# Attention of a gated recurrence with its MLP: from 128-token chunks on the whole tensor array to 64-token sub-chunks on its quarters

## The chip, the cores and the metric

One NeuronCore of one Trainium2 chip runs the program. The metric is device time in microseconds, the median of three executions. Engines named below: TensorE (PE for its products, PEld for its weight loads), VectorE (DVE), ScalarE (ACT), GpSimd (POOL) and SyncE (SP), which issues the transfers.

## The reference

Attention with a decaying state, for 4 batches, 8 heads, 768 tokens and a head size of 48, then one block of token mixing and an MLP (model size 384, hidden size 1536):

```python
for t in range(S):
    kt, vt, rt = (k[:, :, t], v[:, :, t], r[:, :, t])
    cur = np.einsum('bhd,bhe->bhde', u[None] * kt, vt)
    y[:, :, t] = np.einsum('bhd,bhde->bhe', rt, state + cur)
    state = w[None, :, :, None] * state + np.einsum('bhd,bhe->bhde', kt, vt)
...
xt = x.transpose(0, 2, 1)
h = xt @ U @ V
u = x + h.transpose(0, 2, 1)
ch = np.maximum(u @ w_ch1, 0.0) @ w_ch2
return (u + ch).astype(np.float32)
```

x is y with its heads side by side. All data are float32, except that the MLP's weights may arrive as float64.

## The kernel before

A batch is six chunks of 128 tokens. Inside a chunk the recurrence is written as products: r and k are multiplied by powers of the decay w and their inverses (`tables`, the tables `tab`, `tabr`, `tabT`), so that a chunk's output is (masked scores) times v, plus r times the state at the chunk's start, plus a diagonal term with u. For chunk n the functions are:

- `a_load`, `a_load_blocks` (L250, L266): r, k, v with tokens on partitions, and from batch 1 on r and k again as 32 x 32 blocks, which VectorE turns.
- `a_pre` (L288): ks (k times the table) and dv (the diagonal term) on GpSimd.
- `a_tr_r`, `a_tr_k` (L335, L357): r and k with head dimensions on partitions, two heads (96 rows) at a time. From batch 1 on the scores use float32r operands, so r and k are each split into a high and a low part (L351 and L353, L371 and L372). r is spread to a block form (`bm`, zeros in the other head's rows), so that one product gives two heads.
- `a_sc` (L376): the scores, in three float32r products per pair of heads (L388 to L390), in batch 0 one float32 product (L383); then the causal mask (L397).
- `a_sq` (L404): r times the state. `a_av` (L413): masked scores times v, added to it in PSUM, then x (L430).
- `a_su` (L442): k times v for the next state, added and decayed at L457 and L458.
- `a_g`, `g_units`, `c_g`, `c_u`: x times U, and the gates that make u of x. `c_store`, `c_blocks`, `c_turn`: u goes to memory and comes back as blocks that VectorE turns.
- `m_1`, `m_2` (L607, L623): the MLP, in two blocks of 384 tokens and twelve hidden steps of 128, each product as three float32r products on high and low parts. 24 steps of 18 products (L613 to L615, L631 to L633) make a batch.

The order of the work is written by hand as lists of units. Batch 0's attention is merged with the conversion of the first 12 weight units (L833). After it, the loop at L840 places the units of batch b's MLP on a line from 0 to 1 and spreads the units of batch b+1's attention over the first 0.6 to 0.7 of it (`add`, L844). `within` (L654) lets the list of a batch run on into the next batch's first chunks. The program's scheduler works from this order, with the estimated times of each instruction; `queued` ties a unit behind given instructions. PSUM has eight banks: tags mm (2), acc (3), tr, sc and av (1 each).

## Time and profile before

| | |
|---|---|
| time, median of 3 runs | 494.33 us (492.8 to 495.66) |
| profiled execution: span from first to last instruction | 492.1 us |
| mean granted TensorE clock in it | 0.968 |
| TensorE busy, products and loads | 461.5 us and 446.6 us |
| VectorE, ScalarE, GpSimd busy | 303.3, 149.6, 235.6 us |
| DMA | 45.23 MB in 196880 packets |

The profile names instructions by engine and line of the kernel. A row of a group holds: line, engine, operation, output <- inputs, shapes, count, then busy time in us and the mean ns of one, then the idle time ahead of it and what ended that. PE is the matmul, PEld the weight load of the same product. Matmuls are pipelined: the length of one in the trace holds its way through the array, so what a product costs in a stream is the distance of starts. A float32 product stands in the trace as two loads and two matmuls, a float32r product as one of each. Times are from the span's start. The profiled execution's own time beyond its span is not given; the median of the runs lies 2.2 us above it.

### The profile page before, as it was taken

How to read it: one execution, taken by the hardware profiler on the slowest of the kernel's cores; microseconds unless marked ns; L12 is line 12 of the kernel's file. 1: busy time of each engine (PE TensorE's matmuls, PEld its weight loads, DVE VectorE, ACT ScalarE, POOL GpSimd, SP SyncE). 2: the span in 40 equal slices, each digit the busy share in tenths (PEclk: the TensorE clock that was granted, in tenths of full speed). 3: DMA queues.
4: the chain of work that ended last, by engine and by line, in shares of the span. 5: the costliest groups of instructions: out<-in, count | busy, mean ns of one | idle time of the engine just before them, and what ended most of it. 6: DMA issues, size and time to landing. Idle time of an engine off the chain costs nothing.

```text
span 492.1 us, 7932 instructions
## 1 busy us (share of the span) xinstructions
PE 461.5 (94%) x2891; PEld 446.6 (91%) x2891; DVE 303.3 (62%) x543; ACT 149.6 (30%) x290; POOL 235.6 (48%) x227
## 2 busy tenths in 40 slices
PE   7869878979999999999999999999999999999994
PEld 6858757969998989999999999999999999999994
DVE  7998968997788666837677453676672533213112
ACT  3535524434332232333222322323231222211110
POOL 5957565747978571645777602468751021000000
PEclk9977969999999999999999999999999999999998
DMA  9999704554764663676267225542001152001001
GB/s 159 200 312 405 160 17 73 89 82 74 103 113 95 101 102 90 152 107 97 50 96 140 54 66 108 107 75 50 2 0 49 57 113 73 0 1 48 1 0 55
DMA packets 196880, 45.23 MB, mean 92 GB/s; under 512 B 187682, under 2 KB 193571, under 8 KB 196835
## 3 DMA queue, kind: packets, MB, share of 16 engines
q1 hardware_dynamic: 196834, 44.66, 44.2%
q8 instruction: 25, 0.41, 0.4%
q14 instruction: 21, 0.16, 0.1%
HBM read 35.79 MB, written 8.85 MB: 91 GB/s over the span
## 4 chain that ended last, share of the span: by engine, by line
PE 64%; DVE 14%; POOL 7%; issue 6%; SPq 4%; DMA 3%; ACT 1%; DVEq 0%; POOLq 0%; ACTq 0%
PE p L631 8%; PE p L632 8%; PE p L613 8%; PE p L633 8%; PE p L615 8%; PE p L614 8%; PE pav L421 5%; SPq L275 3%; DVE rl L353 2%; PE pav L410 2%; DVE raw_w L189 2%; POOL kT L323 2%; PE psu L449 2%; DVE raw_w L188 1%; POOL dv L295 1%
## 5 line engine op out<-in xcount | busy, mean ns | idle before, releaser
L619 DVE SCALAR_TENSOR_TENSOR hl<-p,hh 128x384 fp32r<-128x384 f32 x96 | 52.6, 549 | 102.1 <-ACT hh L618 102.0
L613 PE MATMUL p<-uTh,w1s 128*128 128x384 f32 x288 | 98.3, 344 | 2.8 <-DVE hl L619 2.5
L631 PE MATMUL p<-w2s,hh 128*128 128x384 f32 x288 | 98.5, 342 | 1.4 <-ACT hh L618 1.4
L614 PE MATMUL p<-uTl,w1s 128*128 128x384 f32 x288 | 97.7, 339 | 1.2 <-DVE uTl L546 1.2
L615 PE MATMUL p<-uTh,w1s 128*128 128x384 f32 x288 | 97.3, 338 | 0.0
L632 PE MATMUL p<-w2s,hh 128*128 128x384 f32 x288 | 96.7, 336 | 0.0
L618 ACT ACTIVATE hh<-p 128x384 fp32r<-128x384 f32 x96 | 46.7, 489 | 148.5 <-PE p L615 147.3
L633 PE MATMUL p<-w2s,hl 128*128 128x384 f32 x288 | 78.8, 338 | 0.1
L613 PEld LDWEIGHTS p<-uTh,w1s 128*128 128x128 f32 x288 | 54.4, 189 | 4.6 <-DVE hl L619 3.7
L631 PEld LDWEIGHTS p<-w2s,hh 128*128 128x128 f32 x288 | 54.2, 188 | 2.6 <-ACT hh L618 2.4
L614 PEld LDWEIGHTS p<-uTl,w1s 128*128 128x128 f32 x288 | 54.6, 190 | 2.0 <-DVE uTl L546 2.0
L615 PEld LDWEIGHTS p<-uTh,w1s 128*128 128x128 f32 x288 | 54.5, 189 | 0.0
L632 PEld LDWEIGHTS p<-w2s,hh 128*128 128x128 f32 x288 | 54.2, 188 | 0.0
L601 POOL TENSOR_TENSOR uTl<-ut,uTh 128x384 fp32r<-128x384 f32 x21 | 21.5, 1025 | 66.6 <-ACT uTh L600 65.2
L633 PEld LDWEIGHTS p<-w2s,hl 128*128 128x128 f32 x288 | 52.5, 189 | 0.5 <-DVE hl L619 0.2
L323 POOL TENSOR_TENSOR kT<-kT,tabT 96x512 f32<-96x512 f32 x18 | 27.3, 1518 | 42.0 <-DVE kT L321 32.7
L421 PEld LDWEIGHTS pav<-ldv,am 128*128 128x128 f32 x320 | 43.4, 198 | 1.5 <-DVE am L397 1.5
L421 PE MATMUL pav<-ldv,am 128*128 128x48 f32 x320 | 42.8, 272 | 0.6 <-DVE am L397 0.5
L397 DVE TENSOR_TENSOR am<-psc,mask 128x512 f32<-128x512 f32 x45 | 30.5, 678 | 9.7 <-PE psc L390 8.0
L353 DVE SCALAR_TENSOR_TENSOR rl<-rT,bm,rh 96x512 fp32r<-96x512 f32 x36 | 34.1, 959 | 3.9 <-ACT rh L351 3.9
L351 ACT ACTIVATE rh<-rT,bm 96x512 fp32r<-96x512 f32 x36 | 24.1, 716 | 22.8 <-POOL rT L323 22.6
L323 POOL TENSOR_TENSOR rT<-rT,tabT 96x512 f32<-96x512 f32 x18 | 24.8, 1379 | 10.8 <-DVE rT L321 10.7
(142 smaller groups left out, 766.6 us busy)
## 6 DMA issues: line engine op xcount, KB each, us to landing
raw_w<-in_moe_w_ch_dram SPq DMA_DIRECT2D x24, 384.0 KB, 7.8
out_dram<-x SPq DMA_DIRECT2D x24, 192.0 KB, 2.1
ud<-x SPq DMA_DIRECT2D x21, 192.0 KB, 2.0
ub<-ud SPq DMA_DIRECT2D x84, 48.0 KB, 2.3
ldr<-in_r_dram SPq DMA_DIRECT2D x20, 192.0 KB, 3.2
ldk<-in_k_dram SPq DMA_DIRECT2D x20, 192.0 KB, 4.0
ldv<-in_v_dram SPq DMA_DIRECT2D x20, 192.0 KB, 3.1
bl<-in_r_dram SPq DMA_DIRECT2D x48, 48.0 KB, 2.4
```

The source lines that it names most:

```text
L323: nc.gpsimd.tensor_mul(xT, xT, tabT[:, i])
L353: nc.vector.scalar_tensor_tensor(rl[:, :, j, :], rT, bm[:, j, 0:1], f32(rh[:, :, j, :]), ALU.mult, ALU.subtract)
L397: nc.vector.tensor_tensor(am, pt.rearrange("p (h t) -> p h t", h=4), mask.unsqueeze(1).broadcast_to([128, 4, C]), ALU.mult)
L421: nc.tensor.matmul(avp[n][:, h * D:(h + 1) * D], lhsT=am[:, hh, :], rhs=vt[:, h, :], start=(c == 0 and h == 0), stop=(h == H - 1), skip_gr ...
L613: nc.tensor.matmul(pt, lhsT=wt[:, 0, fs], rhs=uh[:, ct, :], start=(ct == 0), stop=False)
L614: nc.tensor.matmul(pt, lhsT=wt[:, 0, fs], rhs=ul[:, ct, :], start=False, stop=False)
L615: nc.tensor.matmul(pt, lhsT=wt[:, 1, fs], rhs=uh[:, ct, :], start=False, stop=(ct == NCT - 1))
L618: i_hh = nc.scalar.activation(hh, pt, AF.Relu)
L619: i_hl = nc.vector.scalar_tensor_tensor(hl, pt, 0.0, f32(hh), ALU.max, ALU.subtract)
L631: nc.tensor.matmul(pt, lhsT=hh[:, ts_], rhs=W2[f][:, 0], start=(f == 0), stop=False)
L632: nc.tensor.matmul(pt, lhsT=hh[:, ts_], rhs=W2[f][:, 1], start=False, stop=False)
L633: nc.tensor.matmul(pt, lhsT=hl[:, ts_], rhs=W2[f][:, 0], start=False, stop=(f == NFT - 1))
```

## The change

A chunk of 128 tokens is handled as two sub-chunks of 64, with a state for each. A pair of heads lies on rows 0 to 47 and 64 to 111, so that each head has one half of the array's rows. Every product of the attention then uses 64 rows and 64 columns of the array at most:

- scores only within a sub-chunk (`p_sc`), in float32 for all batches: the splits of r and k and the block form of r are gone, and the mask has 64 columns;
- k times v per sub-chunk (`p_su`), and two states per chunk (`a_st`);
- scores times v and r times the state per sub-chunk (`p_out`). For the second head of each pair v is needed with its two token halves exchanged; `load_swapped` loads it so, in two more transfers per chunk.

A chunk's output is made in two parts (`a_part`): row 0 uses the array's upper rows for the output while the next chunk's second scores and state products use the lower rows; row 1 the other way round. `in_turn` issues the two lists alternately, each product tied behind the one before. Between the two parts stands a product on the whole array (`whole` takes the next MLP product for it, or `between` makes one), and the second part's first product waits for a small ScalarE read of the bank (`see`, `behind`), as both parts write to one bank. `a_first` makes the scores and state products of a batch's first chunk. Chunks are made ready (`ready`) two ahead. A batch's list now begins with its own loads and ends with its last chunk. In batch 0 weight conversions are queued behind the last mask and the last state (`gate`).

```diff
-    PD = 2 * D
+    HP = 64
+    C2 = C // 2
+    PD = HP + D
+    PE_ = 2 * HP
     DM = H * D
...
+    def load_swapped(n):
+        b, c = divmod(n, NCH)
+        t = work.tile([128, NP, D], F32, tag="vsw", name=f"vsw_{n}", bufs=NVS)
+        for i in range(2):
+            s0 = c * C + i * C2
+            nc.sync.dma_start(t[(1 - i) * C2:(2 - i) * C2], v[b, 1::2, s0:s0 + C2, :].rearrange("h p d -> p h d"))
+        vsw[n] = t
+    vsw = {}
...
+    def p_sc(n, j):
+        rT, kT = trs[n]
+        pt = abs_[n][j]
+        rows = head_rows(j)
+        return [lambda q=q, i=i: nc.tensor.matmul(
+            pt[(i ^ j) * C2:(i ^ j) * C2 + C2, q * C2:(q + 1) * C2], lhsT=kT[rows, q, i * C2:(i + 1) * C2],
+            rhs=rT[rows, q, i * C2:(i + 1) * C2], start=True, stop=True) for q in range(NP) for i in range(2)]
+    def p_su(n, i):
+        if n % NCH == NCH - 1 and i:
+            return []
+        ks, vt, dv = pre[n]
+        pt = abs_[n][i]
+        half = slice(i * C2, (i + 1) * C2)
+        hp = HP if n < NCH else D
+        def one(q, j):
+            m = D if j else HP
+            k0 = (2 * q + j) * hp
+            return nc.tensor.matmul(pt[j * HP:j * HP + m, SU + q * D:SU + (q + 1) * D],
+                                    lhsT=ks.rearrange("p h d -> p (h d)")[half, k0:k0 + m],
+                                    rhs=vt[half, 2 * q + j, :], start=True, stop=True)
+        return [lambda q=q, j=j: one(q, j) for q in range(NP) for j in range(2)]
+    def p_out(n, row):
+        am = ams[n]
+        vt = pre[n][1]
+        rT = trs[n][0]
+        pt = avp[n]
+        ps_ = []
+        def to(q, j, i):
+            return pt[i * C2:(i + 1) * C2, (2 * q + j) * D:(2 * q + j + 1) * D]
+        def av(q, j, i):
+            half = slice(row * C2, (row + 1) * C2)
+            return nc.tensor.matmul(to(q, j, i), lhsT=am[j][half, q, :],
+                                    rhs=vsw[n][half, q, :] if j else vt[half, 2 * q, :],
+                                    start=(row == 0 and q == 0), stop=False, skip_group_check=True)
+        def sq(q, i):
+            rows = head_rows(row)
+            return nc.tensor.matmul(to(q, row, i), lhsT=rT[rows, q, i * C2:(i + 1) * C2], rhs=St[n, i][rows, q, :],
+                                    start=False, stop=(row == 1 and q == NP - 1), skip_group_check=True)
+        for q in range(NP):
+            for i in range(2):
+                ps_.append(lambda q=q, i=i: av(q, i ^ row, i))
+        for q in range(NP):
+            for i in range(2):
+                if (n, i) in St:
+                    ps_.append(lambda q=q, i=i: sq(q, i))
+        return ps_
+    def in_turn(last, *lists):
+        for k in range(max(map(len, lists))):
+            for l in lists:
+                if k < len(l):
+                    with ExitStack() as st:
+                        if last is not None:
+                            st.enter_context(tc.issue_after(last.ins))
+                        last = l[k]()
+        return last
+    SU = 4 * C2
...
+    def whole(*args, **kw):
+        if not opened:
+            return nc.tensor.matmul(*args, **kw)
+        with tc.issue_after(opened.pop()):
+            closed.append(nc.tensor.matmul(*args, **kw))
+    def a_banks(n):
+        abs_[n] = [ps_tile(t, f"pab_{n}_{j}", 1) for j, t in enumerate(AB)]
+    def between(n):
+        if opened:
+            whole(avp[n][:, DM:DM + 1], lhsT=ident, rhs=ident[:, :1], start=False, stop=False, skip_group_check=True)
+        return closed.pop()
+    seen = {}
+    def see(n):
+        t = work.tile([128, 1], F32, tag="seen", name=f"seen_{n}", bufs=2)
+        seen[n] = nc.scalar.copy(t[C2:C2 + 1], avp[n][C2:C2 + 1, 7 * D - 1:7 * D])
+    def behind(n, f):
+        def go():
+            i = f()
+            tc.add_manual_dep(i.ins, seen.pop(n).ins.name,
+                              mybir.DependencyInfo(mybir.DependencyClass.Sync, mybir.DependencyReason.DATA),
+                              reason="one bank for both halves of the rows")
+            return i
+        return go
...
+    def a_first(n):
+        a_banks(n)
+        in_turn(None, p_sc(n, 0) + p_su(n, 0), p_sc(n, 1) + p_su(n, 1))
+        ams[n] = [None, None]
+        for j in range(2):
+            a_am(n, j)
+        a_st(n)
+    def a_part(n, row):
+        nxt = (n + 1) % NCH
+        if row == 0:
+            if nxt:
+                a_banks(n + 1)
+            avp[n] = ps_tile("mm", f"pav_{n}", 2) if n < NCH and n % 2 else ps_tile("av", f"pav_{n}", 1)
+        o = 1 - row
+        lists = [p_out(n, row), p_sc(n + 1, o) + p_su(n + 1, o) if nxt else []]
+        if row:
+            lists[0][0] = behind(n, lists[0][0])
+        last = in_turn(between(n) if row else None, *lists)
+        if row == 0:
+            opened.append(last.ins)
+            see(n)
+            if nxt:
+                ams[n + 1] = [None, None]
+        if nxt:
+            a_am(n + 1, o)
+        if row == 0:
+            return
+        a_x(n)
+        trs.pop(n)
+        vsw.pop(n)
+        ams.pop(n)
+        if nxt:
+            a_st(n + 1)
...
+    def a_am(n, j):
+        am = work.tile([128, NP, C2], F32, tag="am", name=f"am_{n}_{j}", bufs=4)
+        i_am = nc.vector.tensor_tensor(am, abs_[n][j][:, :SU].rearrange("p (h t) -> p h t", h=NP),
+                                mask.unsqueeze(1).broadcast_to([128, NP, C2]), ALU.mult)
+        ams[n][j] = am
         if plain(n):
+            gate[:] = [i_am.ins] + gate[1:]
...
+    def a_st(n):
+        for i in range(2):
+            if n % NCH == NCH - 1 and i:
+                return
+            ptv = abs_[n][i][:PD, SU:SU + NP * D].rearrange("p (q e) -> p q e", q=NP)
+            sn = work.tile([PD, NP, D], F32, tag="S", name=f"S_{n}_{i}", bufs=5)
+            if (n, i) not in St:
+                nc.vector.tensor_tensor(sn, ptv, wm, ALU.mult)
             else:
+                nc.vector.tensor_tensor(sn, ptv, St[n, i], ALU.add)
+                i_s = nc.gpsimd.tensor_mul(sn, sn, wm)
+                if plain(n):
+                    gate[1:] = [i_s.ins]
+            St[(n, 1) if i == 0 else (n + 1, 0)] = sn
...
-            return b * NCH <= n < (b + 1) * NCH or b and n < NB
+            return b * NCH <= n < (b + 1) * NCH
...
+        def ready(n):
+            return [lambda: a_pre(n), lambda: a_tr_r(n), lambda: a_tr_k(n)]
+        n0 = b * NCH
+        if b:
+            units += [lambda: (a_load(n0), a_load(n0 + 1))]
+            units += [lambda i=i: (a_load_blocks(n0, i, 0), a_load_blocks(n0, i, 1)) for i in range(4)]
+        if b:
+            units += ready(n0)
+        units += [lambda: a_first(n0)] + ready(n0 + 1)
...
+            def u0(n=n):
+                if b and (n + 2) // NCH == b:
                     a_load(n + 2)
                 bl(n, 0)
+                a_part(n, 0)
+            def u1(n=n):
+                bl(n, 1)
+                if b == 0 and n:
                     a_g(n - 1)
+            def u2(n=n):
                 bl(n, 2)
+                a_part(n, 1)
+                bl(n, 3)
+            units += [u0, u1, u2]
+            if c + 2 < NCH:
+                units += ready(n + 2)
+            if b:
+                units += g_units(n)
             if n == NCH - 1:
+                units += [lambda i=i: c_x(i) for i in range(3)]
...
-    merge(attn_units(0), [f for _, f in wu[:NW0]])
+    merge(attn_units(0), [lambda f=f: queued(f, *gate) for _, f in wu[:NW0]])
```

310 lines of the change are left out of this document (105 added, 205 removed).

## The prediction

> **What bounds the kernel now.** I read the page's engine line first, then a table of busy time by stretch, then TensorE's rows in order of time.
>
> ```profile
> PE 461.5 (94%) x2891; PEld 446.6 (91%) x2891; DVE 303.3 (62%) x543; ACT 149.6 (30%) x290; POOL 235.6 (48%) x227
> ```
>
> ```profile
> 12.00:76.00 64.00, 52.98 (x315) 46.48 (x313) 54.79 (x82) 29.25 (x58) 45.56 (x44) 0.81 0.77 211
> 76.00:199.60 123.60, 114.84 (x719) 109.47 (x719) 98.45 (x171) 42.88 (x85) 79.10 (x71) 0.99 0.57 96
> 199.60:303.90 104.30, 103.70 (x683) 102.82 (x683) 64.22 (x121) 31.54 (x59) 57.47 (x54) 1.00 0.51 94
> 303.90:408.80 104.90, 104.90 (x694) 104.29 (x693) 57.42 (x103) 28.62 (x55) 43.77 (x40) 1.00 0.29 59
> 408.80:492.10 83.30, 76.57 (x442) 76.25 (x440) 19.31 (x36) 13.24 (x27) 3.05 (x3) 0.97 0.07 23
> ```
>
> The columns of the second fence are length, then busy time of PE, PEld, DVE, ACT and POOL, then granted clock, DMA share and GB/s. I cut at the first products of each batch's MLP. The first stretch is batch 0's attention; the next three are an MLP with the next batch's attention beside it; the last is the fourth MLP alone. In the stretches of 104.30 and 104.90 us TensorE never pauses. The one of 123.60 us holds the same products, so about 19 us of it is something else. The question is then what a chunk of attention costs TensorE. The critical chain and the timeline of TensorE price it:
>
> ```profile
> 405.28 0.52 PE p L633 x3
> 408.40 0.52 PE p L633 x3
> ```
>
> ```profile
> 242.15 1.03 PE L410 MATMUL pav<-S,rT 96*128 96x96 f32 x8
> 242.96 0.36 PE L388 MATMUL psc<-rh,kh 96*128 96x256 f32 x1
> ...
> 243.75 0.99 PE L421 MATMUL pav<-ldv,am 128*128 128x48 f32 x8
> ...
> 247.44 0.33 PE L614 MATMUL p<-uTl,w1s 128*128 128x384 f32 x1
> 247.62 0.34 PE L615 MATMUL p<-uTh,w1s 128*128 128x384 f32 x1
> 247.79 0.84 PE L449 MATMUL psu<-ldv,ks 128*96 128x96 f32 x8
> 248.41 0.42 PE L631 MATMUL p<-w2s,hh 128*128 128x384 f32 x1
> ...
> 250.06 0.99 PE L421 MATMUL pav<-ldv,am 128*128 128x48 f32 x8
> 250.87 0.37 PE L388 MATMUL psc<-rh,kh 96*128 96x256 f32 x1
> ```
>
> An MLP step (18 products) repeats every 3.12 us; 24 steps are 74.9 us. Prices of attention are differences of starts: state times r for all pairs 0.81 us (242.15 to 242.96), half a chunk's scores 0.79 (242.96 to 243.75), the state update 0.62 (247.79 to 248.41), half a chunk's scores times v 0.81 (250.06 to 250.87). A batch has six chunks of 2 x 0.79 + 2 x 0.81 = 3.20 us, and five each of 0.81 and 0.62: 19.2 + 7.15 = 26.35 us. Eighteen small products (G and gates) at the 0.175 us of an MLP product add 3.2. Together 74.9 + 26.35 + 3.2 = 104.4 us, against 104.30 measured: the books close, and 26.35 us per batch is what the change rewrites.
>
> **Part 1, the products on quarters.** Per batch the change has 96 products of scores, 96 of scores times v, 88 of state times r and 88 of k times v: 368 products, each float32 and so, like L421 and L449 now, two weight loads with a matmul each (L421 shows x8 for four heads): 736 pairs. They lie in 13 runs (a_first and twelve parts), in which the row half changes with every product and the column half with every second. What a pair costs must be bounded:
>
> ```profile
> L421 PEld LDWEIGHTS pav<-ldv,am 128*128 128x128 f32 x320 | 43.4, 198 | 1.5 <-DVE am L397 1.5
> L449 PEld LDWEIGHTS psu<-ldv,ks 128*96 128x96 f32 x128 | 13.9, 164 | 0.2
> L615 PE MATMUL p<-uTh,w1s 128*128 128x384 f32 x288 | 97.3, 338 | 0.0
> ```
>
> L421 takes 0.81/8 = 0.101 us a pair with 128 weight columns and 48 moving ones; L449 0.62/8 = 0.078 with 96 and 96. The price follows the weight columns, 0.80 ns each, and not the moving ones. So a pair with 64 weight columns is worth 51 ns alone. If quarters run one after another, 736 x 51 = 37.5 us; two at a time, 18.8; all four at a time (13 ns a pair), 9.6. The trace has no product on part of the array. I take 20 ns a pair, between two and four at a time, because the rows at 247.44 and 247.62 show full loads hidden behind streams of 0.17 us, but nothing on how fast short ones can be issued: 14.7 us.
>
> Each run is also entered from and left to a product on the whole array. The trace's nearest price is the tail of a full product: 338 ns long in the L615 row, while the next starts 0.17 us after it, so about 0.17 us is hidden by overlap; a load (164 to 198 ns) is hidden likewise. If both are exposed a change of mode costs up to 0.35 us, and at least nothing. I take 0.25, two per run: 13 x 0.5 = 6.5 us a batch. A batch's attention then takes 14.7 + 6.5 = 21.2 us, and gains 5.1; three batches beside an MLP gain 15.5 us. At 13 ns the gain is 10.3 a batch (31 in all); at 51 ns it is a loss of 17.6 (53). Equal cost lies at (26.35 - 6.5)/736 = 27 ns a pair.
>
> The Trainium skill, "TensorEngine Tiling (Array Packing)", section Key Properties, speaks against the change: a switch of tiling mode drains the engine, even though tiles of one mode run independently. Taken without any drain, my sum would gain 6.5 us more per batch. No row here shows a switch.
>
> The waits inside a part: the second half's first product waits for a one-element copy on ScalarE (`see`), which queues behind the relus there. Behind it on TensorE wait the rest of the part and the MLP. In the list of units the two halves lie two units apart; a batch's 54 units are spread over 0.7 of the MLP's 49, so 1.3 MLP units, each half of 3.12 us, lie between. I count it at nothing; uncovered, it costs up to half a microsecond per chunk (it is far shorter than the 0.72 us of L351, below).
>
> **Part 2, what leaves the other engines.**
>
> ```profile
> L353 DVE SCALAR_TENSOR_TENSOR rl<-rT,bm,rh 96x512 fp32r<-96x512 f32 x36 | 34.1, 959 | 3.9 <-ACT rh L351 3.9
> L397 DVE TENSOR_TENSOR am<-psc,mask 128x512 f32<-128x512 f32 x45 | 30.5, 678 | 9.7 <-PE psc L390 8.0 <-PE psc L383 1.3
> L372 DVE TENSOR_TENSOR kl<-kT,kh 96x512 fp32r<-96x512 f32 x18 | 20.8, 1155 | 0.0
> L457 DVE TENSOR_TENSOR S<-psu,S 96x384 f32<-96x384 f32 x16 | 8.6, 539 | 0.7 <-PE psu L449 0.7
> ...
> L101 DVE TENSOR_TENSOR tabT<-pw,sq 96x256 f32<-96x256 f32 x1 | 0.4, 416 | 0.0
> ```
>
> ```profile
> L351 ACT ACTIVATE rh<-rT,bm 96x512 fp32r<-96x512 f32 x36 | 24.1, 716 | 22.8 <-POOL rT L323 22.6
> ```
>
> With float32 scores the splits go: two rl and one kl, 2 x 0.96 + 1.16 = 3.08 us of VectorE per chunk. The mask works on 256 instead of 512 elements (0.42 for 0.68 us, twice, by L101); the state is added in two pieces of 192 elements (at most 2 x 0.42 for 0.54). Net about 3.3 us of VectorE per chunk, 20 per batch, and over 1.4 us of ScalarE. In the two full stretches this hides behind TensorE and is worth nothing. In the stretch of 123.60 us it isn't hidden; waits there (first fence) and the chain from 80 to 150 us:
>
> ```profile
> PEld p L613 <- DVE hl L619: 3.7, 4, 1.9
> ...
> PEld psc L389 <- DVE rl L353: 2.2, 2, 1.5
> ```
>
> ```profile
> by line: issue 12.1%; DVE rl L353 8.2%; SPq L275 7.9%; SPq L587 5.3%; POOL uTl L601 4.5%; POOL kT L323 4.2%; POOL rT L323 4.2%; DMA out_dram<-x 3.8%; DVE kl L372 3.6%; DVE hl L619 3.4%; DVE raw_w L189 3.0%; POOL w2s L201 2.9%; DMA bl<-in_k_
> ```
>
> rl and kl are 11.8% of 70 us of that chain, 8.3 us. What is late next there are GpSimd's products with the tables and SP's issues, which stay. I take -6 us (0 to -10).
>
> **Part 3, the loads.**
>
> ```profile
> L275 SPq DMA_DIRECT2D bl<-in_r_dram x96: 311/467/1496, 78.5 to 314.3; - x96
> ```
>
> ```profile
> 200.32 2.46 SPq L638 DMA_DIRECT2D out_dram<-x  x3
> 203.00 3.96 SPq L587 DMA_DIRECT2D ub<-ud  x8
> ```
>
> v is loaded a second time with its token halves exchanged: two more issues on SP per chunk, about 0.9 us at 0.467 each. The block loads keep their number. More weighty is `within`: it no longer lets a batch's list run over into the next batch. A batch's first two chunks (10 issues) and its 32 block loads are therefore issued at its own start, behind the output stores and u blocks of the two rows just shown: 42 x 0.467 = 20 us, while now such loads come ahead. MLP products can fill TensorE meanwhile, and the attention has to be packed into what is left. This concerns batches 2 and 3 (batch 1 begins so now too). I take +3 us each, 0 to +16: +6.
>
> **Part 4, the first 76 us.** Scores were float32 there already, so VectorE gains little: the smaller masks pay for a few memsets of padding. On the chain from 30 to 48 us:
>
> ```profile
> 33.60 1.66 PE pav L410 x8
> 35.26 3.33 PE pav L421 x16
> 38.59 3.56 PE psc L383 x8
> ```
>
> ```profile
> 33.60:42.15 8.55, 8.55 (x35) 7.69 (x34) 7.21 (x12) 3.96 (x8) 6.17 (x6) 0.50 1.03 403
> ```
>
> These 8.55 us run at a granted clock of about a half. Quarters shorten them if they overlap, but the state now takes two adds and two GpSimd products in a row per chunk, where one of each stood, and weights are converted only behind the last mask and state. I take +1 (-5 to +6).
>
> **Sum.** 492.1 (the profiled span) - 15.5 - 6 + 6 + 1 = 477.6. The median of the runs, 494.33, lies 2.2 us above the span, so 480 us.
>
> **Rivals.**
> A. Quarters do not overlap, so the change does not do what it says. Place: the 13 runs of every batch; it decides from 27 ns a pair. At 51 ns: 492.1 + 53 - 6 + 6 + 1 + 2.2 = 548; at 35 ns, 736 x 35 + 6500 = 32.3 us a batch, a loss of 17.7 us: 513. For it: 736 pairs replace 248, and no row shows two products side by side. Against it: PEld is busy 102.82 and PE 103.70 of the same 104.30 us, so the engine overlaps at least a load with a product. Chance 0.14, slower.
> B. Batch-start loads: TensorE stands in a_first for 16 us in batches 2 and 3. Price 2 x 13 over my sum: 506. It decides where the list's eight units (5 MLP units, 8 us) end before the 20 us of issues. For it: the SP rows above. Against it: in the stretch of 123.60 us the same late start left PE busy 114.84 us. Chance 0.12, slower.
> C. Four at a time, 13 ns, and VectorE's full relief: 492.1 - 31 - 10 + 1 + 1 + 2.2 = 455, with the loads nearly hidden (+1). For it: TensorE has nothing else to wait for in the two full stretches. Against it: a chain of 736 short pairs needs an instruction issued every 6.5 ns, and the closest matmul starts in these rows are 78 ns apart. Chance 0.17.
> D. Loads overlap only between row halves, two at a time: 736 x 25.5 + 6500 = 25.3 us a batch, gain 1.1; 492.1 - 3 - 6 + 6 + 1 + 2.2 = 492. Chance 0.10. This is the rule of the Trainium skill, "TensorE: Matmul & The Clock Gate", Part 3: a weight load overlaps running products only where the row group differs. By the rows here, one load overlaps a product of the same rows, which goes further than that rule.
>
> **How the numbers follow.** Forecast 0.47, nearly all faster. With C, 0.61 faster, and 0.03 from D; slower are A, B and 0.03 of D: 0.29; within 0.5% (what a measurement can just tell) 0.04 of D and 0.03 of the forecast: 0.07. The range runs from C's 455 to 513, A at 35 ns, with B inside; it leaves A's far end and the best of C outside. The likeliest case's own range is 464 to 490.
>
> **What would show it.** Right: runs of quarter products with starts 15 to 25 ns apart, a part of about 1.6 us between two MLP products, the stretches of 104 us down to about 99 to 102, and the one of 123.60 to about 112; no rl and kl rows. Wrong: starts 35 ns or more apart, PE idle before a_first behind a block load, or PE waiting for `seen` or for the state.

## The result and the profile after

The changed kernel takes 527.84 us (median of four runs, 526.97 to 528.79), against 494.61 of the kernel before beside it: a ratio of 1.0677, interval 1.0649 to 1.0705. It is slower by 33 us where I had forecast a gain of 14, and it lies outside the range. The profiled execution spans 526.9 us, 34.8 more than before.

First the page's engine line and its row of granted clock, for the changed kernel:

```profile
PE 455.8 (86%) x4879; PEld 416.5 (79%) x4879; DVE 243.5 (46%) x525; ACT 112.2 (21%) x247; POOL 230.0 (44%) x246
PEclk8556556996799999999997899999689999999999
```

TensorE has more products and less busy time than before (455.8 against 461.5 us). So the products did not get dearer; the engine stands. VectorE lost 60 us of work, as foretold. The clock row has two dips in its second half, in the two full stretches, where the granted clock was 1.00 before.

The same stretches as in the prediction, cut again at the first products of each MLP (length, then busy time of PE, PEld, DVE, ACT, POOL, then clock, DMA share, GB/s):

```profile
12.00:90.20 78.20, 55.63 (x846) 45.81 (x845) 55.01 (x98) 23.10 (x52) 51.07 (x52) 0.55 0.75 200
90.20:218.40 128.20, 109.47 (x1209) 98.21 (x1210) 69.56 (x152) 30.81 (x69) 71.30 (x72) 0.93 0.58 100
218.40:331.40 113.00, 103.79 (x1173) 93.51 (x1172) 49.40 (x110) 20.98 (x47) 57.26 (x60) 0.95 0.55 104
331.40:443.50 112.10, 102.37 (x1176) 95.49 (x1175) 42.44 (x95) 20.68 (x46) 42.51 (x46) 0.94 0.26 56
443.50:526.90 83.40, 76.65 (x443) 76.33 (x441) 19.30 (x36) 13.24 (x27) 3.09 (x3) 0.99 0.09 27
```

Each stretch with attention in it got longer: the first by 14.2 us (78.20 against 64.00), then 128.20 against 123.60, 113.00 against 104.30, 112.10 against 104.90. The last, with no attention, is unchanged. In the two stretches where TensorE never paused, it now stands for 9.2 and 9.7 us (length less PE busy) and runs at 0.95 and 0.94 of its clock.

What a part of a chunk costs TensorE shows in its timeline; here one part between two MLP steps:

```profile
262.73 0.34 PE L465 MATMUL p<-uTh,w1s 128*128 128x384 f32 x1
263.00 0.25 PE L425 MATMUL pav<-vsw,am 64*64 64x48 f32 x1
...
263.92 0.22 PE L431 MATMUL pav<-S,rT 48*64 48x48 f32 x1
264.07 0.62 PE L465 MATMUL p<-w2s,hh 128*128 128x384 f32 x2
```

Sixty-four pairs start between 263.00 and 263.92: 14.6 ns a pair. The first comes 0.27 us after the last MLP product started, where the next MLP product would have come after 0.17; the next MLP product starts 0.15 us after the last pair. A whole part therefore costs about 1.2 us. That is cheap. Now what TensorE waits for in the stretch 218.4 to 331.4 (wait in all, times, longest):

```profile
PE pG L590 <- POOL xl L550: 3.8, 2, 3.0
PE pav L425 <- DVE am L533: 2.3, 2, 1.6
PE pab L391 <- POOL rT L361: 1.5, 1, 1.5
PE pab L391 <- DVE S L563: 1.2, 1, 1.2
```

These four are 8.8 of the 9.2 us. The longest kind of wait ahead of the first MLP (12 to 90.2) and beside MLP 1 (90.2 to 218.4), in this order, is that of the scores for the state's add (S at L563):

```profile
PE pab L391 <- DVE S L563: 10.9, 4, 4.1
...
PE pav L467 <- ACT seen L483: 1.6, 4, 0.8
```

```profile
PE pab L391 <- DVE S L563: 6.3, 2, 5.6
```

They are of two kinds. xl, am and rT are operands of attention that another engine has yet to make. The scores (pab, L391) have rT and kT for operands and not S: they wait for VectorE's add at L563 to finish reading the PSUM bank that they write. Each half of a chunk has one bank, and the chunk before's state product stands in it; in e6 below, where odd chunks of batch 0 have other banks, the scores' wait for S is gone ahead of the first MLP. During either kind of wait TensorE starts no MLP product. Before the change, its longest wait ahead of the first MLP was that of G's products for x, and none was for the state:

```profile
PE pG L467 <- DVE x L430: 9.2, 3, 4.4
```

A wait for an operand of the changed kernel, step by step, in the timelines of TensorE, GpSimd and VectorE of the next stretch:

```profile
384.30 0.31 PE L425 MATMUL pav<-ldv,am 64*64 64x48 f32 x2
387.97 0.27 PE L391 MATMUL pab<-rT,kT 48*64 48x64 f32 x1 [3.36 <-POOL rT L361]
```

```profile
381.97 1.30 POOL L361 TENSOR_TENSOR kT<-kT,tabT 112x512 f32<-112x512 f32 x1 [5.83 <-DVE kT L359]
383.22 1.02 POOL L330 TENSOR_TENSOR ks<-ldk,tab 128x384 f32<-128x384 f32 x1
384.19 1.00 POOL L333 TENSOR_TENSOR dv<-ldr,ldk 128x384 f32<-128x384 f32 x1
385.14 1.00 POOL L550 TENSOR_TENSOR xl<-x,xh 128x384 fp32r<-128x384 f32 x1
386.09 0.60 POOL L564 TENSOR_TENSOR S<-S,wm 112x192 f32<-112x192 f32 x1
386.64 1.27 POOL L361 TENSOR_TENSOR rT<-rT,tabT 112x512 f32<-112x512 f32 x1
```

```profile
382.78 0.75 DVE L359 STREAM_TRANSPOSE rT<-bl 128x256 f32<-128x256 f32 x2
386.73 0.36 DVE L563 TENSOR_TENSOR S<-pab,S 112x192 f32<-112x192 f32 x1 [3.19 <-POOL S L564]
```

The part has begun with two products of its output and then needs the next chunk's scores, whose r stands last in a burst on GpSimd. GpSimd had been idle for 5.83 us until k was turned, and then worked 6 us without a pause. VectorE's second add of the state waits 3.19 us behind the same burst. TensorE starts nothing for 3.67 us (384.30 to 387.97), and the MLP product that comes after the part (389.10) has no wait of its own.

A wait costs more than its length. The next rows are windows of a stretch of waits, with PE busy for 1.24 of 6.10 us, and of the part that comes right after it:

```profile
280.00:286.10 6.10, 1.24 (x4) 0.51 (x4) 5.55 (x12) 0.90 (x2) 6.10 (x7) 0.75 0.71 124
286.10:287.80 1.70, 1.66 (x46) 1.66 (x46) 0.72 (x2) 0.00 (x0) 1.58 (x3) 0.50 0.96 127
```

Those 46 pairs take 1.66 us, 36 ns each, at a granted clock of 0.50. Over the stretch the records show 10.2 us at half clock, which cost at most 5.1.

With all starts of TensorE between 218.4 and 331.4 the books close: 432 MLP products at 0.1735 us, 74.95; small products 3.2 as before; starts inside the quarter runs 13.6; entering and leaving 21 and 23 such runs at 0.094 and 0.165 us above the normal 0.174 and nothing, 5.8. That is 97.5 us, 6.8 less than before. The waits add about 9.5, the half clock up to 5.1: 112.1 of 113.0.

### The profile page after: what moved, and what is told of

Read it like the earlier page. It is cut to its first block, busy times and chain, and to the rows that moved or that the text cites. A ratio compares the mean times of both kernels' runs of the same rounds, so it can differ in the third digit from the quotient of the medians.

```text
span 526.9 us, 11947 instructions
## 1 busy us (share of the span) xinstructions
PE 455.8 (86%) x4879; PEld 416.5 (79%) x4879; DVE 243.5 (46%) x525; ACT 112.2 (21%) x247; POOL 230.0 (44%) x246
## 4 chain that ended last, share of the span: by engine, by line
PE 64%; SPq 10%; POOL 8%; DVE 8%; issue 4%; DMA 4%; ACT 1%; DVEq 0%; POOLq 0%; ACTq 0%
PE p L465 49%; SPq L309 5%; PE pav L425 3%; PE pav L431 3%; PE pab L391 2%; POOL ks L330 2%; SPq L266 2%; DVE raw_w L195 2%; POOL dv L333 1%; DVE raw_w L194 1%; PE p L467 1%; POOL xl L550 1%; DMA bl<-in_k_dram 1%; POOL rT L361 1%; PE pab L407 1%
## 5 line engine op out<-in xcount | busy, mean ns | idle before, releaser
L465 PE MATMUL p<-uTh,w1s 128*128 128x384 f32 x570 | 163.0, 342 | 1.9 <-DVE x L633 1.6
L465 PE MATMUL p<-w2s,hh 128*128 128x384 f32 x564 | 134.3, 347 | 1.5 <-ACT hh L726 1.2
L391 PE MATMUL pab<-rT,kT 48*64 48x64 f32 x768 | 39.5, 256 | 27.5 <-DVE S L563 18.4
L391 PEld LDWEIGHTS pab<-rT,kT 48*64 48x64 f32 x768 | 31.6, 162 | 36.0 <-issue 15.5
L709 POOL TENSOR_TENSOR uTl<-ut,uTh 128x384 fp32r<-128x384 f32 x21 | 21.4, 1020 | 71.7 <-ACT uTh L708 71.7
L431 PE MATMUL pav<-S,rT 48*64 48x48 f32 x704 | 40.5, 245 | 1.6 <-POOL S L564 1.6
L425 PE MATMUL pav<-ldv,am 64*64 64x48 f32 x320 | 32.8, 241 | 8.3 <-DVE am L533 8.3
L425 PE MATMUL pav<-vsw,am 64*64 64x48 f32 x384 | 38.7, 251 | 0.0
L431 PEld LDWEIGHTS pav<-S,rT 48*64 48x64 f32 x704 | 36.0, 162 | 2.6 <-POOL S L564 2.0
L425 PEld LDWEIGHTS pav<-ldv,am 64*64 64x64 f32 x320 | 25.7, 150 | 14.2 <-DVE am L533 10.1
L425 PEld LDWEIGHTS pav<-vsw,am 64*64 64x64 f32 x384 | 32.0, 162 | 4.8 <-issue 4.0
L564 POOL TENSOR_TENSOR S<-S,wm 112x192 f32<-112x192 f32 x40 | 28.4, 710 | 12.8 <-DVE S L563 12.8
```

The lines of the kernel that those rows point to most:

```text
L391: return [lambda q=q, i=i: nc.tensor.matmul(pt[(i ^ j) * C2:(i ^ j) * C2 + C2, q * C2:(q + 1) * C2], lhsT=kT[rows, q, i * C2:(i + 1) * C2] ...
L425: return nc.tensor.matmul(to(q, j, i), lhsT=am[j][half, q, :], rhs=vsw[n][half, q, :] if j else vt[half, 2 * q, :], start=(row == 0 and q ...
L431: return nc.tensor.matmul(to(q, row, i), lhsT=rT[rows, q, i * C2:(i + 1) * C2], rhs=St[n, i][rows, q, :], start=False, stop=(row == 1 and ...
L465: return nc.tensor.matmul(*args, **kw)
L564: i_s = nc.gpsimd.tensor_mul(sn, sn, wm)
L709: nc.gpsimd.tensor_tensor(ul[:, ct, :], ut, f32(uh[:, ct, :]), ALU.subtract)
```

## The experiments

The lengths by stretch of all runs but e1, taken from the first product, the first product of each MLP and the last (us). The fifth stretch is 76.3 in every one. The second column is the ratio to the kernel before, with its interval.

| run | ratio | before MLP 1 | MLP 1 | MLP 2 | MLP 3 |
|---|---|---|---|---|---|
| before | 1 | 74.5 | 123.4 | 104.3 | 104.9 |
| after | 1.0677 (1.0649 to 1.0705) | 88.7 | 128.2 | 113.0 | 112.1 |
| e2, state on VectorE | 1.0837 (1.0813 to 1.0862) | 88.1 | 130.4 | 113.4 | 116.5 |
| e3, xl on VectorE | 1.0587 (1.0562 to 1.0613) | 87.8 | 126.4 | 112.4 | 110.6 |
| e4, before with float32 scores | 0.9984 (0.9964 to 1.0004) | 73.8 | 120.6 | 107.4 | 106.1 |
| e5, more buffers | 1.0587 (1.0492 to 1.0683) | 91.1 | 130.3 | 107.4 | 105.2 |
| e6, banks in batch 0 | 1.0733 (1.0697 to 1.0769) | 88.7 | 130.5 | 111.6 | 112.0 |
| e7, wake products | 1.0941 (1.0877 to 1.1005) | 95.4 | 132.6 | 113.6 | 112.4 |
| e8, loads a batch ahead | 1.0709 (1.0671 to 1.0748) | 88.6 | 129.2 | 117.0 | 106.5 |
| e9, pairing undone | 1.0505 (1.0425 to 1.0586) | 87.1 | 127.3 | 108.1 | 107.0 |
| e10, e9, e5 and e3 together | 1.0645 (1.0614 to 1.0676) | 88.3 | 136.7 | 112.7 | 102.7 |
| e11, late conversions | one run | 100.3 | 131.3 | 111.8 | 111.5 |
| e12, no swapped loads in batch 0 | 1.0775 (1.0679 to 1.0870) | 87.7 | 130.7 | 112.7 | 112.6 |
| e13, e9 and e12 together | 1.0476 (1.0401 to 1.0550) | 86.2 | 130.5 | 107.9 | 104.5 |

Stretches that an edit doesn't touch move too. e6, e7, e11 and e12 edit what is ahead of the first MLP alone, and in them MLP 1 is 2.3 to 4.4 us longer, while MLP 2 and 3 stay within 1.4; between e9 and e13, MLP 3 moves by 2.5. I build nothing on less.

### What a quarter product costs by itself (e1)

At the end of the changed kernel stand streams of products that nothing reads: in rotation over the four quarters, alternating row halves, alternating column halves, on one quarter, on the whole array, and in rotation again.

```diff
+    stream([lambda k=k: nc.tensor.matmul(**quarter(k, *order[k % 4])) for k in range(800)])
+    stream([lambda k=k: nc.tensor.matmul(**quarter(k, k % 2, 0)) for k in range(400)])
+    stream([lambda k=k: nc.tensor.matmul(**quarter(k, 0, k % 2)) for k in range(400)])
+    stream([lambda k=k: nc.tensor.matmul(**quarter(k, 0, 0)) for k in range(200)])
...
```

> The changed kernel with products appended behind its last MLP product, which nobody reads: 800 on the four quarters in rotation, 400 alternating between row halves, 400 alternating between column halves, 200 on one quarter, 100 on the whole array (128 x 48), then 800 in rotation again; each is two pairs. Theory W (TensorE waits for the attention's data, and the granted clock falls only because it stands): the clock stays at 1.0 through every stream, the rotation runs at 14 to 15 ns a pair (23 us for 800 products). Theory Q (products on quarters do not count as full activity, and themselves lower the clock): the clock is 0.5 for most of the streams on quarters and the rotation takes 26 to 28 ns a pair. On overlap: if all quarters load on their own, row halves and column halves both take about 26 ns a pair and one quarter about 52; if loads overlap only between row halves, column halves take 52.

The time was 743.31 us. First a row of TensorE's timeline in the rotation, then windows of the rotation, the row halves, the column halves, one quarter, and whole-array products of 128 by 48:

```profile
535.19 2.08 PE L978 MATMUL s<-ident 64*64 64x48 f32 x128 [1.65 <-issue]
```

```profile
528.50:545.00 16.50, 9.64 (x608) 9.13 (x602) 0.00 (x0) 0.00 (x0) 0.00 (x0) 0.99 0.02 5
565.00:588.00 23.00, 23.00 (x799) 23.00 (x794) 0.00 (x0) 0.00 (x0) 0.00 (x0) 1.00 0.02 4
588.00:611.50 23.50, 23.50 (x814) 23.50 (x810) 0.00 (x0) 0.00 (x0) 0.00 (x0) 1.00 0.02 5
617.00:650.00 33.00, 33.00 (x313) 33.00 (x311) 0.00 (x0) 0.00 (x0) 0.00 (x0) 0.50 0.00 1
651.00:693.00 42.00, 42.00 (x198) 41.95 (x197) 0.00 (x0) 0.00 (x0) 0.00 (x0) 0.50 0.00 1
```

The rotation runs in bursts of 128 pairs at about 14.7 ns a pair and then stands for some 1.9 us, with no wait but "issue" (15.7 us in 11 stops). Counted with its stops, a pair takes 27 ns in this window (16.50 us for 608) and 28.6 over the whole stream. The instruction queue's packets explain the stops: the page of this run has 82 of them, 42 more than the changed kernel, and 2,700 products of two loads and two matmuls are 10,800 instructions, 257 for each packet. So 128 pairs are one packet's worth. In the trace a packet of 16 KB ends 1.2 to 1.6 us ahead of each burst (at 530.23, 533.83 and 537.63 us, with bursts from 531.47, 535.19 and 539.20). This stream runs at the rate of instruction fetch. In the kernel itself a part has 64 pairs with long products around it, and the "issue" waits there are 0.3 us at most in the MLP stretches. Rival A's condition, 27 ns a pair or more, is met only by a stream that the kernel doesn't have.

One quarter alone takes 105 ns a pair at half clock. Its first 80 pairs, before the clock fell, start every 58 ns, 7 more than the 51 that I had worked out from the weight columns. Row halves and column halves both come at 29 ns, evenly and without a stop: half of 58, as the 14.7 of a burst are about a quarter of it. So quarters work beside one another whether they share rows or columns, and rival D, by which column halves would take as long as one quarter, is out. (29 is also close to the 28.6 that the packets allow, so halves might be faster than this with more instructions at hand; the run can't tell.)

Neither theory about the clock holds as it was put: the halves kept 1.00, one quarter fell to 0.50 without a pause, and the rotation, at 0.99 in this window, had 3.4 and 6.8 us at half clock on either side of it.

### Is VectorE's relief worth anything? (e4)

The kernel before with float32 scores in every batch: the splits rl and kl go, the rest stays.

```diff
-            nc.vector.scalar_tensor_tensor(rl[:, :, j, :], rT, bm[:, j, 0:1], f32(rh[:, :, j, :]),
-                                           ALU.mult, ALU.subtract)
...
-        nc.vector.tensor_tensor(kl, kT, f32(kh), ALU.subtract)
```

> The kernel before with float32 scores in all batches, as batch 0 has them: one part of the change alone, without quarters. The splits of r and k into high and low parts go, 3.1 us of VectorE per chunk; scores take 8 products of about 0.215 us per chunk where 12 took 1.58 us, so TensorE gets 0.1 to 0.2 us per chunk more, 1 us a batch. If the relief of VectorE is worth the 6 us that the prediction gave it: 488 to 491. If it is worth nothing: 495 to 498.

It took 494.49 us: no change, between the two ranges expected. Its three MLP stretches:

```profile
75.50:196.00 120.50, 113.81 (x676) 108.86 (x677) 74.66 (x148) 39.99 (x80) 75.73 (x72) 0.97 0.59 100
196.00:303.40 107.40, 107.40 (x676) 105.60 (x675) 51.33 (x105) 27.65 (x53) 54.55 (x53) 1.00 0.50 91
303.40:409.60 106.20, 106.20 (x671) 104.75 (x670) 44.65 (x88) 24.62 (x48) 41.11 (x40) 1.00 0.27 57
```

VectorE's busy time in the first falls from 98.45 to 74.66 us and the stretch from 123.4 to 120.6. In the two full ones float32 products on the whole array cost TensorE 3.1 and 1.2 more. If they cost as much in the first, the relief there is worth 4 to 6 us by this estimate, near the 6 of my sum; but 2.8 us is no more than MLP 1 moves by itself, what is gained is given back elsewhere, and in the changed kernel other waits take its place.

### Which operands, and why late (e2, e3, e5, e8)

In e2 the state's product with wm goes to VectorE, in e3 the split of x.

```diff
-                i_s = nc.gpsimd.tensor_mul(sn, sn, wm)
+                i_s = nc.vector.tensor_mul(sn, sn, wm)
```

```diff
-        nc.gpsimd.tensor_tensor(xl, x, f32(xh), ALU.subtract)
+        nc.vector.tensor_tensor(xl, x, f32(xh), ALU.subtract)
```

> The changed kernel with the decay of the state (two per chunk) on VectorE instead of GpSimd. Theory W, in the form that the chain from the output's second half to the next chunk's first half is what TensorE waits for, and that the state stands in GpSimd's queue behind the work that makes later chunks ready: the waits of the scores for the state's second add (10.9 us before the first MLP, 6.3 in the stretch after it) mostly go, and the time falls by 8 to 20 us, to 507 to 519. If the late block loads are what it waits for instead, or if the price is the clock under quarters, the time stays within 4 us of 527.

> The changed kernel with x's low part (xl) made on VectorE instead of GpSimd. The products of G waited 3.8 and 2.9 us for it in the stretches beside the second and third MLP, and the clock was a half for 10 us right behind the longest of these waits. Theory W: both go, 6 us of waits and some 10 us of lost clock together at most: 512 to 522. If a wait only passes to the next late operand of the same chunk, 524 to 530.

e2 came to 535.6 us, worse than the change and outside both ranges expected; e3 to 523.23, better by 4.6 and between the two. The rows that took the place of the ones removed, TensorE's waits in e2 before the first MLP and in e3 beside MLPs 2 and 3:

```profile
PE pav L467 <- ACT seen L483: 11.2, 5, 3.2
```

```profile
PE pav L425 <- DVE am L533: 5.4, 4, 2.5
PE pab L391 <- POOL rT L361: 5.0, 2, 2.7
PE pab L391 <- POOL dv L336: 3.4, 1, 3.4
```

In e2 the scores' wait for S goes from 10.9 us to 1.1, and 11.2 appear for `seen`, which had 1.6 in the changed kernel. In e3 the 6.7 us of waits for xl fall to 2.8, and am, rT and dv take over. So neither of these two operations on GpSimd is the cause alone: where one is relieved, another step of the same parts is late. Both edits also lengthen VectorE's queue, and that share isn't separated.

e5 asks whether buffers hold the operands back. It has three buffers for rT, and reuses the tiles of r and k for dv and ks so that those aren't held either (the table is kept for 64 tokens to make room).

```diff
-    NRK = 4
+    NRK = 7
...
-        rT = work.tile([PE_, NP, C], F32, tag="rT", name=f"rT_{n}", bufs=2)
+        rT = work.tile([PE_, NP, C], F32, tag="rT", name=f"rT_{n}", bufs=3)
...
+        dv = xpool.tile([128, H, D], F32, tag="hh", name=f"dv_{n}", bufs=NH) if n < NCH else rt
```

> The changed kernel with room to prepare chunk n+2 while chunk n is in work: a third buffer for r turned (rT), and from batch 1 on dv and ks written over the loaded r and k, of which seven tiles are kept instead of four (the double copy of the decay table goes to make room). Theory B (buffers): r turned for chunk n+2 takes the buffer that the second half of chunk n's output reads, and must be there for the first half of chunk n+1, whose lists hold the scores of n+2; dv waits for x of chunk n in the same way, and GpSimd's queue stands behind both. Then the waits of the scores for rT and of later steps in the two stretches beside the second and third MLP fall from about 10 us each to under 4, the clock falls less, and the time drops by 10 to 25 us, to 502 to 517. If the queue behind x and the state is what counts, not the buffers, the time stays within 4 us of 527.

It took 522.46 us, 5.4 less than the change and between the two ranges expected. In the windows of MLPs 2 and 3:

```profile
223.00:330.50 107.50, 103.72 (x1174) 94.16 (x1173) 48.31 (x109) 21.19 (x47) 57.14 (x60) 0.95 0.56 108
330.50:435.70 105.20, 100.93 (x1176) 94.02 (x1175) 41.26 (x92) 20.77 (x46) 37.68 (x41) 0.97 0.25 55
```

TensorE's idle time there falls from 9.2 and 9.7 us to 3.8 and 4.3, and the stretches by 5.6 and 6.9. Of its waits over both stretches, first two rows of the changed kernel, then the longest of e5:

```profile
PE pG L590 <- POOL xl L550: 6.7, 3, 3.0
PE pab L391 <- POOL rT L361: 6.0, 3, 3.4
```

```profile
PE pav L436 <- DVE am L544: 4.3, 3, 2.2
```

In e5 none is left for rT, and 0.6 us for xl. This is the clearest part of the cause: with two buffers, rT of chunk n+2 can be written only when the last part of chunk n has read its own, and one chunk later it is needed as the first thing of the output part of n+1. Before, a chunk's output needed nothing of the next chunk. Which of the buffers that e5 frees counts most is not separated.

e8 issues the loads of batches 2 and 3 during the MLP before, which takes away what I had priced at +6 (and rival B at 26 more).

```diff
-        if b:
-            units += [lambda: (a_load(n0), a_load(n0 + 1))]
-            units += [lambda i=i: (a_load_blocks(n0, i, 0), a_load_blocks(n0, i, 1)) for i in range(4)]
+        if b == 1:
+            units += load_units(b)
...
+            if b + 2 < B:
+                add(load_units(b + 2), 6, end, 0.9)
```

> The changed kernel with the first loads of batches 2 and 3 (two chunks and their blocks) queued late in the batch before, as it was before the change. Theory L (rival B of the prediction: TensorE stands at a batch's start for its loads): the stretches beside the second and third MLP fall by 5 us each or more, to under 517 in all. If their waits lie in the middle of a batch, as the trace of the changed kernel shows them, the time stays within 3 us of 527.

It took 528.48 us, nothing gained over both stretches together (223.5 against 225.1): MLP 3 is 5.6 shorter and MLP 2 4.0 longer, for a reason that the run doesn't show. In sum the late batch loads cost nothing that loading earlier gets back, and none of TensorE's waits in these stretches of the changed kernel is for a load.

### Undoing the pairing (e9, e10)

e9 keeps the quarters, but makes a chunk's scores and state products in a run of their own, in the unit between the two output parts. So a part needs its own operands alone; but the next chunk's scores still stand ahead of the second part in the list.

```diff
-        lists = [p_out(n, row), p_sc(n + 1, o) + p_su(n + 1, o) if nxt else []]
+        lists = [p_out(n, row)]
...
+                if (n + 1) % NCH:
+                    a_first(n + 1)
```

> The changed kernel with one part undone: the next chunk's scores and state products no longer stand beside the output's halves, but run by themselves between the two halves (as a_first does for a batch's first chunk). Quarters stay. An output run then has one half of the rows only (28 to 30 ns a pair by the streams, 0.9 us for 32 pairs), so TensorE has some 1 us more per chunk. Theory C (coupling): TensorE stands because an output half cannot start before the chunk behind it is ready, and the scores cannot start before the output's operands are; then the first x comes nearer to 19 us (29 now), the stalls over 0.6 us (72 us in all) fall by 20 us or more, and the time to 500 to 515. If the waits lie in the queues whatever stands beside what: 525 to 545.

It took 519.3 us, 8.5 less than the change and above the 500 to 515 of the theory. Its two runs lie 6.4 us apart (516.11 and 522.49), and the profile is that of the faster. Windows of MLPs 2 and 3, and the longest of TensorE's waits in them:

```profile
216.10:324.20 108.10, 105.00 (x1192) 96.95 (x1192) 50.41 (x111) 20.99 (x47) 56.57 (x59) 0.98 0.56 104
324.20:431.20 107.00, 105.52 (x1176) 98.51 (x1175) 41.99 (x95) 20.60 (x46) 42.75 (x46) 0.97 0.30 62
```

```profile
PE pav L425 <- DVE x L533: 1.7, 1, 1.7
```

Idle time is 3.1 and 1.5 us. The runs that were interleaved in one part are now separate, and their starts cost more (17 us a batch inside the runs against 13.6), yet the stretches get shorter by about 5 each: the waits cost more than the overlap of the two lists gained. How much of this is the joining and how much the other place of the next chunk's scores and state is not separated.

e10 has three edits: e9's, e5's and e3's (xl on VectorE).

> The same, with the room for three chunks (e5_three_buffers) and xl on VectorE (e3_xl_dve). If the three causes add up, 8 to 12 us below e9_uncoupled; a version that beats the kernel before would be under 492. If buffers matter only where output and scores are coupled, within 4 us of e9_uncoupled.

The gains don't add. It took 526.48 us, 7.2 more than e9 and neither of the two outcomes expected, as MLP 1 rose to 136.7 (127.3 in e9), where the scores again wait 7.2 us for the state's add, and MLP 2 to 112.7 (108.1). But its last window shows the products when nothing is late:

```profile
339.20:441.90 102.70, 102.47 (x1170) 95.44 (x1169) 44.17 (x98) 20.58 (x46) 33.16 (x35) 1.00 0.25 57
```

TensorE is busy for all but 0.23 us, at full clock, and the stretch is 2.2 us shorter than before: the direction of my forecast, for one stretch of three, but within what this stretch moves without an edit to it.

### The 14 us ahead of the first MLP (e6, e7, e11, e12, e13)

Five edits, each against one explanation. In e6 odd chunks of batch 0 take their scores' banks from the pool of accumulators; in e7 six whole-array products that add into unread columns keep the clock up in each part; in e11 the conversions of the weights, all but one, come behind batch 0's attention; in e12 batch 0's swapped copies of v aren't loaded (its odd heads multiply a table); e13 is e9 with e12.

```diff
+        if n < NCH and n % 2:
+            abs_[n] = [ps_tile("acc", f"pab_{n}_{j}", 3) for j in range(2)]
+            return
```

```diff
+            for _ in range(6 if plain(n) else 0):
+                with tc.issue_after(closed.pop().ins):
+                    closed.append(nc.tensor.matmul(avp[n][:, DM:], lhsT=ident, rhs=ident, start=False, stop=False,
+                                                   skip_group_check=True))
```

```diff
-    merge(attn_units(0), [lambda f=f: queued(f, *gate) for _, f in wu[:NW0]])
+    merge(attn_units(0), [lambda f=f: queued(f, *gate) for _, f in wu[:1]])
+    for _, f in wu[1:NW0]:
+        queued(f, *gate)
```

```diff
+        if n < NCH:
+            vsw[n] = tab[:, :NP * D].rearrange("p (q d) -> p q d", d=D)
+            return
```

> The changed kernel with a second pair of PSUM banks for scores and state before the first MLP (odd chunks use two of the accumulators' banks, which are free there). Theory F1 (banks): before the first MLP TensorE waits 10.9 us for the second add of the state, only because the next scores go to the same bank; these go, and the stretch before the first MLP falls from 88.7 by 8 to 12 us: 515 to 519. If the chain goes through the state itself or through the conversion of weights on VectorE, the stretch falls by under 3 us: 524 to 527.

> The changed kernel with six products that nobody reads (128 x 128, float32) between the two halves of each of batch 0's six chunks, 1.3 us a chunk at the full clock and 2.6 at half. Theory F2 (clock): the stretch before the first MLP is long because TensorE has so little to do there that it is granted half its clock for 72 of 89 us; with more to do the clock rises and the stretch falls by 5 us or more, to under 84. If its length comes from waits and the clock is only a sign of them, the stretch gets longer by 3 to 12 us.

> The changed kernel with 11 of the 12 weight conversions of the stretch before the first MLP moved behind batch 0's attention. Theory F3 (conversions in VectorE's and ScalarE's queues, waiting for their transfers, stand between the attention's own steps): the last x of batch 0, at 82.9 us now, comes at 62 us or before; the conversions then follow, so the whole need not gain. If the attention's own chain sets the pace: the last x at 75 us or later.

> The changed kernel, but the first batch's swapped copies of v are not loaded (48 KB, twice for each of its 6 chunks); its odd heads multiply a table in their place, so their outputs are of other numbers. Front theory L (the added loads, of 192 bytes a packet, delay all loads behind them in SP's queue while the DMA engines are busy): the front falls from 88.7 us to 80 or less, the last x comes at about 75 instead of 82.9, and the time is about 519. Rival F (the order of products, VectorE and GpSimd sets the front's pace, not the loads): the front stays within 2 us of 88.7 and the time within 3 of 527.

> The kernel with the next chunk's scores and state products in runs of their own (as in the run that undid the pairing: 519.3, front 87.1), and without the first batch's swapped loads of v (its odd heads multiply a table instead). Theory L: its front falls by 7 or more below 87.1, also if the pairing hid that in the changed kernel, and its time to about 511. Rival F: the front stays at 85 to 89 and the time at 516 to 522.

None shortened it by more than 2.5 us. TensorE's waits there in e6 and e11, then the window of e7:

```profile
PE pav L467 <- ACT seen L486: 13.8, 4, 7.2
```

```profile
PE pav L431 <- POOL S L564: 10.9, 1, 10.9
```

```profile
12.00:97.40 85.40, 58.21 (x914) 49.09 (x912) 54.52 (x99) 24.13 (x53) 50.96 (x51) 0.72 0.68 183
```

e6 (529.65 us): the waits for S go, `seen` takes their place, and the length is the same. e7 (539.89): the clock rises from 0.55 to 0.72 and half-clock time falls from 71.7 to 47.8 us, yet the stretch is 6.7 us longer. The added products themselves take TensorE some 14 us in the trace, so a gain of a few us from the clock could hide behind them; that the low clock only follows from the standing is argued and not shown. e11 (541.74): up to the fifth output x is at most 4.2 us earlier than in the changed kernel, and 1.9 for the fifth (72.25 us against 74.19), so the conversions explain little of the 14 us as far as that. Then the stretch grows to 100.3, as the last chunk waits for a state behind a product on GpSimd (dv, L339) that the trace records as 10.9 us long, 0.8 otherwise, while VectorE works through the postponed conversions. e12 (532.12) and e13 (517.34): 87.7 and 86.2 us, so the added loads aren't it either (e12's whole time lies 2 us above the range expected for that). What stays is the order in the engines' queues, argued and not shown. VectorE's row for the first chunk's output, of the kernel before and of the changed one, then the last products of this output and its row in e9:

```profile
19.28 0.54 DVE L430 TENSOR_TENSOR x<-pav,dv 128x384 f32<-128x384 f32 x1
```

```profile
29.01 0.55 DVE L542 TENSOR_TENSOR x<-pav,dv 128x384 f32<-128x384 f32 x1
```

```profile
21.26 1.05 PE L431 MATMUL pav<-S,rT 48*64 48x48 f32 x8
...
29.64 0.54 DVE L533 TENSOR_TENSOR x<-pav,dv 128x384 f32<-128x384 f32 x1
```

9.7 of the 14 us are there with the first chunk. Its last product ends at 25.13 us (17.88 before), and x starts 3.9 us after that (1.4 before), behind VectorE's sum over a later chunk's dv, which had waited 1.85 us for GpSimd. In e9 and e13 the products of this output end earlier, at 22.31 and 17.36 us, the latter as early as before the change; but x starts at 29.64 and 28.10, as VectorE works through masks, states and conversions first. So undoing the pairing helps TensorE there and not x, and the last x of the batch comes at 83.7 and 82.9 us, as in the changed kernel (82.9; 68.8 before). No run has the edits of e13 and e11 together. Which link of that chain is the late one I haven't settled.

## Why the prediction was wrong, step by step

**Part 1's price was near; its use failed.** I had 20 ns a pair and two mode switches of 0.25 us for 13 runs: 21.2 us a batch. Measured are 13.6 us of starts and 5.8 for the switches, 19.4 together, as the cheaper pairs (rival C's price) meet more and cheaper switches (some 22 runs, as a_first comes in pieces, at 0.26 us for in and out together). That the two sums lie so close is partly luck: a quarter alone is dearer than I had it (58 ns for 51), but four work at a time, and the runs are more and each switch cheaper. The Trainium skill, "TensorEngine Tiling (Array Packing)", section Key Properties, says that a switch of tiling mode drains the engine. The trace agrees that a switch costs something, 0.094 us going in and 0.165 coming out, half of what I took. So TensorE's own work fell by 6.8 us per full stretch, more than the 5.1 that I had counted.

**The step that failed** is the one after it: that these stretches stay bound by TensorE's work, and that waits inside a part count at nothing. I priced one such wait (`seen`, 1.6 us here before the first MLP, none over a microsecond) and named "PE waiting for the state" only among the signs of error. The change makes one in-order run of two chunks' products: for each part the output's operands (am, S, v), the next chunk's (rT, kT, ks) and the bank that the next chunk's scores write must all be ready, and TensorE starts no MLP product meanwhile. With rT in two buffers, one bank for each half and the state's add behind other work, they come late. The two full stretches pay 9.2 and 9.7 us of standing and up to 5 and 7 for half clock, more than the 6.8 that the products gained. e9 and e5 support the joining and the buffers as causes there, by taking 4.9 to 6.9 us out of each of these stretches, and e2 and e3 show that neither of two operations is it alone. These two stretches are 15.9 of the 34.8 us that the span grew by; 14.2 lie ahead of the first MLP (part 4). That e10 has one stretch without a wait and is 8.5 us longer than the change in another says that the order of the rest decides which; why the state's add is late in its MLP 1 isn't settled.

**Part 2** may have had about the right size (4 to 6 us by the estimate from e4, 6 in the sum) but is not gained: MLP 1 is 4.8 us longer, as TensorE stands there in waits of the same kinds (6.3 us for the state's add).

**Part 3** was wrong in place. The +6 for batch loads bought nothing back in e8, no wait of TensorE in these stretches is for a load, and rival B falls with it.

**Part 4** said +1 for the first stretch; it is +14. This term is the most mis-sized of the sum. I had argued there with TensorE's price at half clock, while in e7 a higher clock didn't shorten it. The cause stays open: the banks (e6) and the added loads (e12) alone are excluded, the conversions (e11) explain little as far as the fifth output, the clock (e7) isn't settled, and undoing the pairing (e9) didn't bring the last x forward.

**The signs.** Starts 15 to 25 ns apart (14.6) and no rl or kl rows came true, near enough; a part came at 1.2 us for 1.6. The stretches didn't: 113.0 and 112.1 us for 99 to 102, and 128.2 for 112. "PE waiting for the state" was the sign of the error that came true (10.9 us before the first MLP and 6.3 beside MLP 1), though for the state's add to free a bank, and not for the state as an operand. None of the rivals had this mechanism. A and D, whose price was the products, were wrong although the time is nearer to A's 513 than to 480: that is chance.

## What to carry to other kernels

On a TensorE that never pauses, the price of its products is half of the question. The other half is when each operand of an in-order run is ready: joining two chunks' products into one run makes the run wait for the latest of all their operands and banks, and everything behind it waits too. So list, for each joined run, which engine makes each operand, behind what it queues there, and when its buffer and the bank that the run writes come free, and count that before the gain; then try the cheaper products without the joining.

## What the hardware showed that I had not expected

- Quarters of the array, in float32, work beside one another: 58 ns a pair on one quarter at full clock, 29 on two that share rows or share columns, 14.7 in the bursts of a rotation over four (e1).
- That rotation, kept up, was bound by instruction fetch: 128 pairs (256 instructions, one packet of 16 KB) in some 1.9 us, then about as long a stop, 28.6 ns a pair over all (e1).
- The granted clock went to 0.50 in streams in which TensorE never paused (one quarter, 33 us; 128 by 48 on the whole array, 42 us), while streams alternating between halves kept 1.00. So work that follows a wait isn't the only case of a low clock; these two streams without a pause are another.
- A change between quarter and whole-array products cost 0.094 us going in and 0.165 coming out, in the changed kernel's stretch from 218.4 to 331.4 us.
